# Loads of one batch reordered, and late divisions and sums moved: a fused linear-attention and feed-forward kernel

## The chip, the core and the metric

The kernel runs on one core of a Trainium2 chip. The engines are named as in the profile: PE (matmul), DVE (vector), ACT (scalar), POOL (GpSimd) and SP, which only issues DMAs here. Each engine works through its own instruction queue in order and waits on semaphores that other engines or landed DMAs raise. The metric is the device time of one execution in microseconds (us). Six runs of the kernel before gave a median of 920.74 us, from 919.83 to 923.76.

## The reference

Two stages, all in float32. The attention has no softmax: each head multiplies k and v into a 64 by 64 matrix, q is multiplied by it, and each row is divided by its root mean square. The result, seen as 4608 tokens of 512 values, goes through a two-layer network with a leaky ReLU.

```
kv  = einsum('bhsd,bhse->bhde', k, v)            # 8 batches, 8 heads, 576 rows, 64 wide
out = einsum('bhsd,bhde->bhse', q, kv)
rms = sqrt(mean(out * out, axis=-1) + 1e-6)
x   = (out / rms * g_norm) -> (4608, 512)
h   = x @ w_in                                   # 512 x 2048
out = maximum(0.01 * h, h) @ w_out               # 2048 x 512
```

## The kernel before

**Blocks.** The 4608 tokens are nine blocks of 512. While block i goes through the network, the attention of batch i+1 is done piecemeal between its matmuls. Since a batch has 576 rows, it ends in the block after the one it begins in. PE's order is written out: every matmul is pinned with `tc.keep_in_program_order`. On the other engines an instruction is pinned only where the code says so (`in_turn` pins when `steady` is set, which is from block 2 on; weight rounding, L242 to L256, is always pinned), and a scheduler puts the rest where it finds a place.

**Block 0** (`first_block`) uses plain matmuls: sixteen column groups n, each h(n) (`h_ps`, then a Prelu on ACT, line 1016) and, one step later, o(n) (`o_acc`). Between them `between(n, half)` does two things. It advances other work by one step (`steps`), and it loads and rounds weights. A weight tile comes by DMA and is rounded by two ACT instructions (L242 "add", L245 "cut") and four DVE ones (L247, L251, L253, L256). Weight tile 2n-1 serves h(n) and tile 2n+2 serves o(n). Rounding runs ahead, up to tile 31.

**Batch 1 inside block 0** is `attention(1, False)`, a generator that `steps` advances. For each half m of the heads it transposes two pairs of q (`turn`, line 426, DVE), multiplies k and v of two pairs (`attention_kv`, `kv_ps` on PE), and in half 0 it issues the loads of the third and fourth pairs (`load_pair`: k and v at line 130, q as four pieces at line 159, all on SP's queue). After half 1 come the copy of kv (line 322, DVE) and two tails. A tail is q times kv (`o_ps` on PE), squares and scaled copies on ACT (lines 350 and 356, or 395 and 400), sums of the squares on DVE (line 354 or 397), and the division. `divide` is a chain that goes to and fro: DVE transposes (line 364) and reduces (365) the sums, ACT takes the root (368), DVE the reciprocal (372), ACT spreads it (376), DVE transposes it back (382) and multiplies x (384). The division of the first tail (rows 576 to 1023, which are in block 1) falls in step n=12. The second tail's squares and sums fall in n=13, and its division is taken up in block 1 by `go(late, 1)`.

**Block 1 and later** use two levels of Strassen-like sums (seven products for eight). Their sums are made on POOL and DVE (`add`, line 598). `sides_x` makes those of x, `combine` and `sides_w1` those of the weights. From block 2 on `product_h_two` gives each of the four chunks c its h products, and the last adds of a chunk make g11, g12, g22 and g21, which ACT's Prelu (line 794) and POOL's sums (`sums_of`) take up. `product_o` does the o products of the chunk before, one step each time `go_o` is called, so that the DVE adds of both stand in one queue.

DMAs use the semaphores of eight lanes in turn, so an SP load waits until the load eight issues back has landed.

Of the kernel before, what the change touches and what calls it, by code (L numbers as in the profile page):

```python
# [23 lines left out]
def kernel(  # L24
# [46 lines left out]
    NB = B * S // NT  # L71
    N2 = NT // 2
    U = 2
    NC = DF // 2 // (U * P)
# [13 lines left out]
    ps_m = ctx.enter_context(tc.tile_pool(name="ps_m", bufs=1, space=bass.MemoryType.PSUM))  # L88

    pin = tc.keep_in_program_order  # L90
    steady = first_done = False

    def in_turn(ins):

        if steady:
            pin(ins)


# [38 lines left out]
    to_load = collections.deque()  # L137
# [281 lines left out]
    def attention(b, apart=True, fine=False):  # L419

        qT = qTs[b] = work.tile([P, NP, S], F32, tag="qT", name="qT")
        kv_ps = kv_tiles()

        def turn(p):
            q_in = q_ins.pop((b, p))
            in_turn(nc.vector.transpose(
                qT[:, p, :].rearrange("p (t s) -> p s t", s=T),
                q_in.rearrange("p (s d) -> p s d", d=D)[:, :, :32]))

        for m in range(2):  # L430
            turn(2 * m)
            yield
            turn(2 * m + 1)
            if m:
                yield
            attention_kv(b, m, kv_ps)
            pairs_next = [(b + m, p) for p in ((2, 3) if m == 0 else (0, 1)) if b + m < B]
            if apart or m == 0:
                for nxt in pairs_next[:1 if apart else 2]:
                    if apart:  # L440
                        to_load.extend((*nxt, what) for what in ("q", "kv"))
                    else:
                        load_pair(*nxt)
            yield
            if apart:
                if m:
                    copy_kv(b, kv_ps)
                for nxt in pairs_next[1:]:
                    to_load.extend((*nxt, what) for what in ("q", "kv"))
                yield  # L450
        if not apart:
            copy_kv(b, kv_ps)
            yield
        tails = [tail_of(b, max(i * NT, b * S), min((i + 1) * NT, (b + 1) * S), fine)
                 for i in (b, b + 1)]
        if not fine:
            for tail in tails:
                yield from tail
            return

        for tail in (0, 0, 0, 0, 0, 1, 0, 0, 1, 1, 1, 1, 1, 1):
            next(tails[tail])
            yield
# [133 lines left out]
    def add(eng, out_, a, b_, minus=False, pinned=False):  # L597
        ins = eng.tensor_tensor(out_, a, b_, op=ALU.subtract if minus else ALU.add)  # L598
        if pinned or steady:
            pin(ins)  # L600
# [291 lines left out]
    def product_h_two(i, c, quarters, to, second):  # L892

        n0 = 7 * ((i - 2) * NC + c)

        into = {1: (0, True), 2: (0, False), 6: (1, True), 5: (3, True), 7: (3, False),
                3: (1, False), 4: (2, True)}
        banks = {}
        for t, k in enumerate(ORDER):
            for js, tags, q in zip(GROUPS, (("ha", "hc"), ("hb", "hd")), (qa, qc)):  # L900
                tag = tags[0 if k in (1, 6, 7, 4) else 1]
                if k in FRESH:
                    banks[tag] = ps_m.tile([P, 4, P], F32, tag=tag, name=f"h_{tag}")
                for n, j in enumerate(js):
                    matmul(banks[tag][:, n, :], lhsT=w_place(n0 + t)[:, AT[j], :],
                           rhs=quarters[k][j], start=k in FRESH and n == 0, stop=True,
                           skip_group_check=True)
                if len(js) < 4 and second:
                    second.product(k, banks[tag][:, 3, :])
                at, fresh = into[k]  # L910
                bank = banks[tag][:, :len(js), :]
                if fresh:
                    nc.scalar.copy(q[:, at], bank)  # L913
                else:
                    add(nc.vector, q[:, at], bank, q[:, at])
                if len(js) < 4 and second:
                    second.done(k, banks[tag][:, 3, :])
            read(n0 + t + 1 + RING)
            yield
        g11, g21, g22, g12 = g_of(c)  # L920
        add(nc.vector, g21, qa[:, :, 0, :], qa[:, :, 1, :])
        add(nc.vector, g11, qa[:, :, 0, :], qc[:, :, 0, :])
        yield
        add(nc.vector, g22, g21, qa[:, :, 2, :])
        add(nc.vector, g12, g22, qa[:, :, 3, :])
        yield
        add(nc.vector, g22, g22, qc[:, :, 1, :])
        add(nc.vector, g21, g21, qc[:, :, 1, :])
        add(nc.vector, g21, g21, qc[:, :, 2, :])
        for t in (g11, g12, g22, g21):  # L930
            relu(t)
        sums_of(c, to)
# [47 lines left out]
    def go(steps, n=None):  # L980
        while n is None or n > 0:
            if next(steps, steps) is steps:
                return
            n = None if n is None else n - 1
# [55 lines left out]
    loaded, rounded = 7, 5  # L1040

    def between(n, half):
        nonlocal loaded, rounded
        go(steps.get(2 * n + half, iter(())), 1)

        while half and rounded < min(3 * n + 8, 2 * n + 13, len(w_jobs) - (n < 11)):
            if loaded < len(w_jobs):
                load_w(loaded)
                loaded += 1
                if loaded in (15, 19):  # L1050
                    load_pair(1, (loaded - 15) // 4)
            round_w(rounded)
            rounded += 1
        if (n, half) == (12, 0):
            for p in range(2):
                load_pair(2, p)

    first_block(between)
    first_done = True
# [35 lines left out]
    for i in range(1, NB):  # L1095
# [4 lines left out]
        for c in range(NC):  # L1100
# [3 lines left out]
            for t in range(7):  # L1104
                slot = 7 * c + t
                go(h_steps, 1)
                if not one:

                    if t == 6:
                        go(h_steps, 1)  # L1110
                    if slot in LATE_SLOTS:
                        go(late, 1)
                    for _ in range(FINE_SLOTS.get(slot, 0)):
                        go(a_steps, 1)
                    if i + 1 < NB:
                        if slot == 20:
                            x_sides, new_quarters, sums, inner = sides_x(i + 1)
                        if slot in (20, 21, 22):
                            go(sums, 2 if slot == 20 else 1)
                        if slot == 24:  # L1120
                            inner(0)
                        elif slot == 25:
                            inner(1)
                    load_some()

                now = (i - 1) * NC + c
                if now - 1 in seconds:
                    for half in range(2):
                        if t == (6 if half else 4):
                            inner_g((now - 1) % NC, half)  # L1130
                    if t == 5 and now <= 2 * NC:
                        inner_w2((now - 1) % NC)
                if slot == 4 and not one:
                    while writes:
                        pin(nc.sync.dma_start(*writes.pop()))
                if slot in HELD and i == NB - 1:
                    pass
                elif waited == LAG:
                    go_o()
                elif o_queue:  # L1140
                    waited += 1
                if one:

                    if t == 1:
                        combine(c, 2)
                    if t == 3 and c < NC - 1:
                        h_sides, more_h = sides_w1(c + 1)
                        combine(c + 1, 0)
                    if t == 5 and c < NC - 1:
                        more_h()  # L1150
                        combine(c + 1, 1)
                    if slot == 4:
                        go(late, 1)
                    if slot in A_SLOTS:
                        go(a_steps, 1)
                    load_some()
                    if slot == 24:
                        go(a_steps)
                        x_sides, new_quarters, sums, inner = sides_x(i + 1)
                        go(sums)  # L1160
                    elif slot == 25:
                        inner(0)
                    elif slot == 26:
                        inner(1)
            if i == NB - 1 and c == NC - 1:
                go(h_steps, 1)
                go_o()
            go(h_steps)
# [42 lines left out]
```

## Time and profile before

| | |
|---|---|
| median of 6 runs | 920.74 us |
| the profiled execution | 921.92 us, of which the span is 920.1 us |
| PE busy | 909.8 us (99% of the span) |
| DVE, ACT, POOL busy | 634.1, 329.3, 370.9 us |
| granted PE clock | 1.00 throughout |
| DMA | 200.06 MB, 217 GB/s over the span |

The span runs from the first to the last instruction of the program; the profiled execution's own time is 1.8 us longer. PE is the busiest engine by far, so a change is worth what it takes from, or adds to, the few places where PE stands still. Times in the views are us from the start of the span. "Idle before <-releaser" says how long the engine stood still ahead of an instruction and what ended that wait.

### The profile page before, as it was taken

To read this page: it belongs to the slowest core of one execution; us is meant where nothing else is said; L and a number is where in the kernel's file an instruction comes from. 1 tells how busy PE (TensorE), PEld (TensorE's weight loads), DVE (VectorE), ACT (ScalarE), POOL (GpSimd) and SP (SyncE) were. 2 spreads that over 40 slices of the span, in tenths; PEclk is the share of its full clock that TensorE was granted. 3 is DMA by queue.
4 is the path that set the end of the run, shared out by engine and by line. 5 is a ranking of instruction groups with operands and counts; after the bars stand their busy time and mean duration, and the time that the engine had idled before them with its cause. 6 is when DMAs were issued, how large, how long until landed. Compare 5 with 4: busy or idle time off the path is not lost.

```text
span 920.1 us, 18028 instructions
## 1 busy us (share of the span) xinstructions
PE 909.8 (99%) x6990; PEld 777.1 (84%) x6990; DVE 634.1 (69%) x1160; ACT 329.3 (36%) x649; POOL 370.9 (40%) x438
## 2 busy tenths in 40 slices
PE   8999999999999999999999999999999999999998
PEld 5444447888998999899999999999999999999997
DVE  5876995587457876687757875687569755755565
ACT  5454533242135233532343323342343333223330
POOL 2000354977633572236222632264226522642222
PEclk9999999999999999999999999999999999999999
DMA  8999936895498679856987599758765676667632
GB/s 254 235 250 224 247 106 193 267 302 166 163 343 265 185 220 294 266 178 196 295 237 230 180 285 270 227 176 251 239 182 175 189 221 199 186 186 222 199 102 92
DMA packets 90229, 200.06 MB, mean 217 GB/s; under 512 B 9888, under 2 KB 42272, under 8 KB 90144
## 3 DMA queue, kind: packets, MB, share of 16 engines
q1 hardware_dynamic: 79680, 187.04, 68.5%
q10 hardware_dynamic: 10016, 10.69, 3.3%
q8 instruction: 56, 0.92, 0.4%
q0 software_dynamic: 448, 1.18, 0.3%
q14 instruction: 29, 0.24, 0.1%
HBM read 172.39 MB, written 26.48 MB: 216 GB/s over the span
## 4 chain that ended last, share of the span: by engine, by line
PE 86%; DMA 9%; DVE 2%; POOL 1%; ACT 1%; issue 1%; SPq 0%; ACTq 0%; POOLq 0%; DVEq 0%
PE o_a L118 18%; PE o_c L118 17%; PE h_ha L118 11%; PE h_hb L118 10%; PE h_hc L118 8%; PE h_hd L118 8%; PE o_acc L118 3%; PE h_ps L118 2%; PE o_ps L118 2%; DMA stage<-in_moe_w_in_dram 2%; DMA pairs<-in_moe_w_out_dram 2%; PE kv_ps L118 2%; DMA v_in<-in_v_dram 1%; PE h_a L118 1%; DMA pairs<-in_moe_w_in_dram 1%; PE h_c L118 1%
## 5 line engine op out<-in xcount | busy, mean ns | idle before, releaser
L598 POOL TENSOR_TENSOR gs<-g 128x512 f32<-128x512 f32 x64 | 82.1, 1283 | 250.6 <-ACT g L794 248.5
L794 ACT ACTIVATE g<-g 128x512 f32<-128x512 f32 x124 | 78.4, 632 | 131.0 <-DVE g L598 131.0
L913 ACT COPY w_all<-h_ha 128x512 f32<-128x512 f32 x84 | 49.0, 583 | 171.5 <-PE h_ha L118 165.9
L118 PE MATMUL o_a<-pairs,gs 128*128 128x256 f32 x384 | 91.3, 381 | 0.0
L118 PE MATMUL o_c<-pairs,gs 128*128 128x256 f32 x376 | 89.6, 381 | 0.0
L598 DVE TENSOR_TENSOR o<-h_hb,o 128x128 f32<-128x128 f32 x104 | 29.9, 288 | 83.5 <-ACT pairs L913 83.5
L598 DVE TENSOR_TENSOR o<-o_c,o 128x512 f32<-128x512 f32 (+1 forms) x91 | 61.3, 673 | 27.6 <-PE o_c L118 27.3
L118 PEld LDWEIGHTS o_a<-pairs,gs 128*128 128x128 f32 x384 | 69.8, 190 | 10.9 <-POOL pairs L598 3.1
L118 PEld LDWEIGHTS o_c<-pairs,gs 128*128 128x128 f32 x376 | 68.3, 190 | 7.9
L598 DVE TENSOR_TENSOR o<-o_a,o 128x512 f32<-128x512 f32 x75 | 51.3, 684 | 29.1 <-PE o_a L118 28.8
L598 POOL TENSOR_TENSOR pairs<-w_all 128x512 f32<-128x512 f32 x8 | 11.1, 1382 | 121.1 <-DMA stage<-in_moe_w_in_dram 93.4
L118 PE MATMUL h_ha<-stage,w_all 128*128 128x128 f32 x448 | 59.6, 276 | 0.0
L118 PEld LDWEIGHTS h_ha<-stage,w_all 128*128 128x128 f32 x448 | 56.6, 192 | 3.0 <-issue 0.9
L118 PE MATMUL h_ps<-xT,w_all 128*128 128x512 f32 (+1 forms) x136 | 57.7, 569 | 0.7 <-DVE xT L560 0.7
L118 PE MATMUL o_acc<-w,g 128*128 128x512 f32 x128 | 57.8, 595 | 0.0
L598 POOL TENSOR_TENSOR pairs<-g 128x128 f32<-128x128 f32 x52 | 24.2, 465 | 82.0 <-PE h_hb L118 52.8
L598 DVE TENSOR_TENSOR g<-g,pairs 128x512 f32<-128x512 f32 x84 | 55.6, 689 | 1.9
L118 PEld LDWEIGHTS h_ps<-xT,w_all 128*128 128x128 f32 x136 | 25.5, 190 | 29.5 <-issue 26.3
L118 PEld LDWEIGHTS o_acc<-w,g 128*128 128x128 f32 x128 | 24.0, 190 | 29.8 <-issue 29.4
L598 DVE TENSOR_TENSOR w_all<-h_hc,w_all 128x512 f32<-128x512 f32 x56 | 38.4, 685 | 14.1 <-PE h_hc L118 13.8
L598 DVE TENSOR_TENSOR o<-h_hd,o 128x128 f32<-128x128 f32 x78 | 22.2, 284 | 36.7 <-ACT pairs L913 36.2
L118 PE MATMUL h_hb<-stage,w_all 128*128 128x128 f32 x336 | 46.7, 275 | 0.0
(225 smaller groups left out, 2267.7 us busy)
## 6 DMA issues: line engine op xcount, KB each, us to landing
w_all<-w SPq DMA_DIRECT2D x196, 448.0 KB, 4.3
pairs<-w SPq DMA_DIRECT2D x56, 512.0 KB, 4.3
out_dram<-o ACTq DMA_DIRECT2D x35, 256.0 KB, 5.4
v_in<-in_v_dram SPq DMA_DIRECT2D x29, 288.0 KB, 5.1
k_in<-in_k_dram SPq DMA_DIRECT2D x28, 288.0 KB, 5.2
q_in<-in_q_dram SPq DMA_DIRECT2D x56, 144.0 KB, 6.1
q_in<-in_q_dram SPq DMA_DIRECT2D x56, 140.0 KB, 6.1
w<-stage SPq DMA_DIRECT2D x12, 512.0 KB, 4.4
```

The lines of the kernel that those rows point to most:

```text
L118: pin(nc.tensor.matmul(*args, **kw))
L598: ins = eng.tensor_tensor(out_, a, b_, op=ALU.subtract if minus else ALU.add)
L794: nc.scalar.activation(t, t if src is None else src, func=AF.Prelu, alpha=SLOPE)
L913: nc.scalar.copy(q[:, at], bank)
```

## The change

Five edits:

- In half 0 of `attention(1, False)` k and v of the third and of the fourth pair are issued first, and then q of both. Before, it was k, v, q of the third and then k, v, q of the fourth.
- `in_turn` also pins when a new flag `in_line` is set. `between` sets it while it advances `steps` for n of 12 and more: the first tail's division and the second tail's sums then stay in program order among the pinned DVE instructions, behind the rounding of all weight tiles.
- The second tail's division is taken up at slot 5 of block 1, not at slot 4, and is pinned too.
- `product_h_two` yields once more, ahead of the last two adds of g21.
- At the very last chunk `go(h_steps, 1)` and `go_o()` are called twice and not once, so that an o add comes between the last adds.

```
-    steady = first_done = False
+    steady = first_done = in_line = False
     def in_turn(ins):
-        if steady:
+        if steady or in_line:
             pin(ins)
...
             if apart or m == 0:
-                for nxt in pairs_next[:1 if apart else 2]:
-                    if apart:
-                        to_load.extend((*nxt, what) for what in ("q", "kv"))
-                    else:
-                        load_pair(*nxt)
+                for nxt in pairs_next[:1] if apart else ():
+                    to_load.extend((*nxt, what) for what in ("q", "kv"))
+                if not apart:
+                    for what in ("kv", "q"):
+                        for nxt in pairs_next:
+                            load_pair(*nxt, what)
...
         add(nc.vector, g22, g22, qc[:, :, 1, :])
+        yield
         add(nc.vector, g21, g21, qc[:, :, 1, :])
         add(nc.vector, g21, g21, qc[:, :, 2, :])
...
     def between(n, half):
-        nonlocal loaded, rounded
+        nonlocal loaded, rounded, in_line
+        in_line = n >= 12
         go(steps.get(2 * n + half, iter(())), 1)
+        in_line = False
...
-                    if slot == 4:
+                    if slot == 5:
+                        in_line = True
                         go(late, 1)
+                        in_line = False
...
-            if i == NB - 1 and c == NC - 1:
+
+            for _ in range(2 if i == NB - 1 and c == NC - 1 else 0):
                 go(h_steps, 1)
                 go_o()
             go(h_steps)
```

## The prediction

> **What bounds the kernel now.** I read the PE waits first, because PE is 99% busy. PE stands still for few causes; the three that the edits touch are these (total us, times, longest).
>
> ```profile
> PE kv_ps L118 <- DMA v_in<-in_v_dram: 1.9, 1, 1.9
> ...
> PE h_b L118 <- ACT g L819: 0.4, 1, 0.4
> ...
> PE o_c L118 <- DVE o L598: 0.4, 1, 0.4
> ```
>
> Next the chain that ended last (start, us, what), to see which waits set the end. v of batch 1's fourth pair is on it at 81.42. So is v of batch 2's fourth pair at 164.83. The h_b wait at 159.56 is not: there the chain runs through POOL's sums and SP.
>
> ```profile
> 81.42 8.08 DMA v_in<-in_v_dram
> 89.50 0.14 issue
> 89.63 1.27 PE kv_ps L118 x70
> ...
> 164.83 5.65 DMA v_in<-in_v_dram
> 170.48 0.04 issue
> 170.53 1.27 PE kv_ps L118 x70
> ```
>
> SP's timeline shows the loads that move: four pieces of q of the third pair stand ahead of k and v of the fourth.
>
> ```profile
> 77.08 2.23 SPq L159 DMA_DIRECT2D q_in<-in_q_dram  x4
> 79.63 0.35 SPq L130 DMA_DIRECT2D k_in<-in_k_dram  x1
> 81.42 0.35 SPq L130 DMA_DIRECT2D v_in<-in_v_dram  x1
> 82.94 3.02 SPq L159 DMA_DIRECT2D q_in<-in_q_dram  x4
> ```
>
> DVE's timeline decides the case. From 100.80 to 140 DVE is idle for one wait of 1.58 us only. Its operations are stretched where POOL adds run: L253 takes 1.76 here and 0.69 elsewhere, while the transposes (L382) keep their 0.63.
>
> ```profile
> 100.80 0.60 DVE L247 TENSOR_SCALAR cut<-cut 128x512 f32<-128x512 f32 x1
> ...
> 123.04 1.76 DVE L253 SCALAR_TENSOR_TENSOR w<-cut,w 128x512 uint32<-128x512 uint32 x1
> ...
> 128.67 0.63 DVE L382 STREAM_TRANSPOSE inv<-spread 128x448 f32<-128x448 f32 x1
> ...
> 131.34 1.21 DVE L256 CUSTOM_DVE_ANT_0 w<-w,add 128x1024 uint16<-128x1024 uint16 x1
> ```
>
> ACT's timeline: the second tail's square waits for that transpose. The Prelus of h(14) at 130.18 and h(15) at 135.35 stand behind it, and both are early or on time.
>
> ```profile
> 129.39 0.39 ACT L395 ACTIVATE sq<-o_ps 128x256 f32<-128x256 f32 x1 [5.27 <-DVE inv L382]
> 129.67 0.62 ACT L400 ACTIVATE xT<-o_ps,g_sb 128x128 f32<-128x128 f32 x2
> 130.18 0.61 ACT L1016 ACTIVATE g<-h_ps 128x512 f32<-128x512 f32 x1
> 135.35 0.60 ACT L1016 ACTIVATE g<-h_ps 128x512 f32<-128x512 f32 x1 [4.57 <-PE h_ps L118]
> ```
>
> **What the Trainium skill says.** "SBUF — State Buffer", section "Who interferes with whom": DVE and POOL share a pair of ports under an exclusive lock; a DVE operation with two SBUF inputs or in a two-port mode, and a POOL one that reads SBUF, block each other for a whole instruction. The trace agrees: L253's 1.76 is the end of a POOL add (124.25) plus 0.55. "PSUM — Partial Sum Buffer", section "Engine vs sequencer instructions": the queues of ACT, DVE and POOL are strict FIFO, and matmuls start in program order. So a Prelu behind a waiting square is late, however ready; the trace shows it at 130.18. "DMA: Bandwidth & Descriptors", section "Queues, rings and completion order": descriptors are consumed in ring order, but completion is not promised in order. Here k, v and q take about the same 6 to 8 us from issue to landing, so I take landings in issue order.
>
> **Edit 1, the loads.** k or v is 288 KB, a pair's q 568 KB (twice 144 + 140). The windows give 254 and 210 GB/s around 80, so 230 in the mean: q takes 2.5 us. Moved ahead of one q, v lands at 89.50 - 2.5 = 87.0. PE comes to these matmuls at 87.41 and stood until 89.63, so 2.2 us of PE go (the waits view books 1.9, the modelled end of two matmuls being later). The k and v buffers were released by matmuls at 70.1, so SP can issue at 77.08, where q stood. q of the third pair lands 2.6 us later, still with that of the fourth; both are first read at 98.24, seven or so us after landing. The bytes in total are the same, so the weights behind them move little. If the landing is not in order, the gain is anything down to 0.
>
> **Edit 2, what the scheduler made of it.** PE's order is the same in both kernels. On ACT the Prelus of h(10) and h(11) and the four `o_ps` instructions of the first tail now come ahead of the rounding of tile 25; before, tiles 25 and 26 were rounded at 98.50 between the two Prelus. All DVE rounding now precedes the division. I follow the chain.
>
> - PE's first-tail products move from 104.77 to 102.57. ACT took from 105.86 to 107.77 for their squares and copies; now 103.66 to 105.57. The two ACT roundings (107.77 to 109.00 before, for tile 27) then end at 106.80, and DVE starts tile 25 at 106.84, not 100.80. DVE's transposes end at 100.95 in both, so nearly 6 us of a full DVE are lost.
> - DVE's work up to the second inverse transpose: 100.80 to 132.55 is 31.75, less the 1.58 wait, less the second multiply (1.61, which now comes after): 28.56. This gives 135.4.
> - Nothing covers the trips to ACT any more: root 0.32 and one spread 0.56 with some 0.2 of semaphores: 1.1. This gives 136.5.
> - The lock: 16 POOL adds (5 from 99.83, 11 from 122.15) fall in the stretch in both kernels. Before, some met transposes or the wait and cost nothing. Alone, the 28.56 would be about 21.5 (seven tiles at 2.25, the rest 5.8), so the lock cost 7. If every add cost its full price (8 large ones at 1.0, 8 small at 0.5) it would be 12. So the extra is 0 to 5, and below 0 by some 2 if adds fall on DVE's waits. With rounding in one piece, I take 1.2: the second inverse transpose ends at 137.7.
> - ACT then: squares and copies of the second tail, 0.9 for each half (129.39 to 130.30), the first half from 0.55 before that transpose's end; then the Prelu of h(15), 0.6, now behind them. It ends 1.8 after the transpose, at 139.5.
> - o(15) starts on PE at 139.55. Before: 135.32 + 3.43 = 138.75. PE itself would have been there at 136.55. So PE stands 3.0, and block 1 begins 0.8 later than before: edit 1's gain is spent.
>
> x is needed by block 1's first matmuls 3.4 us after that; the second multiply and the sums of x (some 2.5 us) fit.
>
> **Edit 3, slot 5.** DVE's h_c add comes ahead of the small division, so ACT's copy at 158.85 is not held up and the 0.43 wait goes. It pays nothing: PE only arrives earlier at the kv matmuls, whose v is set by POOL's sums that start when h_c ends (149.1), SP's queue and the landing at 170.48. h_d's add, now behind the division, has until 163.09.
>
> **Edits 4 and 5, the end.** Now DVE does three g adds (898.38 to 900.39) and then the o_c add (900.31 to 900.99); PE's next o_c matmuls wait for it from 900.69 to 901.14. With one g add ahead the o_c add ends at 899.7, and the 0.45 goes. The last g add ends 0.6 later, POOL's four sums likewise (second one at 904.4), but PE needs that one at 907.7. After that PE runs to the end: -0.45 is in full. Its cover gone, the same wait would stand elsewhere, down to 0.
>
> **Sum.** +0.8 + 0 - 0.45 = +0.35. The profiled execution's own 921.92 would be 922.3. It lies 1.2 above the median of the runs shown and within their spread, so I put the same +0.35 on the median: 921.1.
>
> **The rivals.** (a) Faster: the division is in time. It needs the inverse transpose by 134.75, so the lock must cost 1.75 less than before, not 1.2 more. Then -2.2 - 0.45 gives 918.1. For it: PE is otherwise full, and POOL's adds may fall on DVE's waits; against it: 6 us less of DVE. (b) Slower: POOL's adds meet rounding one for one. From an inverse transpose at 139.2 on (an extra of 2.7) the kernel is more than 0.2% slower; at an extra of 3.4 o(15) starts at 141.75, +3.0 - 0.45, 923.3. For it: eleven POOL adds follow each other from 122.15, right where rounding now stands undivided. (c) The loads don't do what they say: v lands as late as before, PE keeps its wait, and the lost DVE time comes on top, all 2.2 later: 923.3. Against it: q's pieces land within 7 us of their issue.
>
> **How the numbers follow.** About 0.2% (1.8 us) is what a measurement can tell from no change. Forecast 0.57 (its own range 919.3 to 922.5), (a) 0.14, (b) 0.23, (c) 0.06. So faster 0.14, same 0.57, slower 0.29. The range takes in most of (a) and all of (b) and (c): 918.6 to 923.8.
>
> **What would show it.** Right: no PE wait on `v_in` near 87; DVE idle for 5 to 6 us from 101; a new PE wait ahead of `o_acc` near 137 of about 3 us, ended by ACT's Prelu, with squares (L395) and DVE's L382 before it; the h_b wait gone but kv_ps still held by v near 171; no o_c wait near 900. Wrong: no wait ahead of the last `o_acc` (then a), one of over 5 us (then b), or a wait that I don't see in block 1's first sums.

## The result and the profile after

The changed kernel takes 927.11 us in the median of 16 runs (925.77 to 928.9), the kernel before 920.93 of 35 on the same chips. The ratio is 1.0064, 95% interval 1.0054 to 1.0075: slower by 5.0 to 6.9 us. The prediction, 921.1 with a range of 918.6 to 923.8, was wrong. The profiled execution of the changed kernel took 926.33 us, with a span of 924.6, 4.5 above the span before.

PE's waits in the changed kernel (total us, times, longest). Those for `v_in`, h_b and o_c, shown of before, are gone. In their place stands one.

```profile
PE o_acc L118 <- ACT g L1018: 5.3, 1, 5.3
```

The chain of waits shown of before went through v's landing twice. After, it goes through neither: from 107.26 on it runs along DVE's rounding and the division to ACT's squares, copies and Prelu, and from there to o(15).

```profile
142.25 5.89 PE o_acc L118 x8
```

SP's timeline: k and v of the fourth pair are issued ahead of q (the window ends ahead of the eighth piece of q).

```profile
75.57 0.33 SPq L130 DMA_DIRECT2D k_in<-in_k_dram  x1
76.12 0.33 SPq L130 DMA_DIRECT2D v_in<-in_v_dram  x1
76.68 6.36 SPq L159 DMA_DIRECT2D q_in<-in_q_dram  x7
```

PE's timeline shows their products, 72 instructions in one piece where before two stood apart from 70, and then o(14), o(15) and the first h_a of block 1. First the o products and that h_a of before, then the changed kernel:

```profile
135.16 7.03 PE L118 MATMUL o_acc<-w,g 128*128 128x512 f32 x16
142.02 1.89 PE L118 MATMUL h_a<-xT,w_all 128*128 128x256 f32 x8
```

```profile
87.84 1.28 PE L118 MATMUL kv_ps<-v_in,k_in 64*64 64x64 f32 x72
...
133.37 3.60 PE L118 MATMUL o_acc<-w,g 128*128 128x512 f32 x8
142.25 5.89 PE L118 MATMUL o_acc<-w,g 128*128 128x512 f32 x8 [5.29 <-ACT g L1018]
147.98 1.89 PE L118 MATMUL h_a<-xT,w_all 128*128 128x256 f32 x8
```

The line of 142.25 and the one after it hold the loss. A group of eight such matmuls takes 3.43 us from its start to the next start (before, sixteen took 6.86). So PE is ready for o(15) at 136.80, the start of o(14) plus 3.43, and starts at 142.25. Then the eight matmuls take 5.73 us, start to start.

DVE's timeline: it is idle from 101.45 and takes up tile 25 at 107.26. Its operations are stretched while POOL adds run (L253 takes 1.64 against 0.69 elsewhere, and ends 0.55 after the POOL add that started at 108.78), and the second inverse transpose ends at 140.55.

```profile
107.26 0.43 DVE L247 TENSOR_SCALAR cut<-cut 128x512 f32<-128x512 f32 x1 [5.81 <-ACT cut L245]
...
109.14 1.64 DVE L253 SCALAR_TENSOR_TENSOR w_all<-cut,w_all 128x512 uint32<-128x512 uint32 x1
...
138.22 0.65 DVE L382 STREAM_TRANSPOSE inv<-spread 128x448 f32<-128x448 f32 x1 [0.63 <-ACT spread L376]
...
139.91 0.64 DVE L382 STREAM_TRANSPOSE inv<-spread 128x448 f32<-128x448 f32 x1
```

```profile
108.78 1.45 POOL L599 TENSOR_TENSOR pairs<-w 128x512 f32<-128x512 f32 x1
110.31 1.59 POOL L599 TENSOR_TENSOR pairs<-w,pairs 128x512 f32<-128x512 f32 x1
```

ACT's timeline: the rounding (L242) stands behind the squares of the first tail (L350), and the Prelu of h(15) at 141.57 behind the squares and copies of the second, which wait for DVE.

```profile
104.08 0.98 ACT L350 ACTIVATE sum<-o_ps 128x448 f32<-128x448 f32 x2 [0.39 <-PE o_ps L118]
...
105.98 0.69 ACT L242 ACTIVATE add<-pairs 128x512 uint32<-128x512 uint32 x1
...
140.02 0.39 ACT L395 ACTIVATE sq<-o_ps 128x256 f32<-128x256 f32 x1 [1.37 <-DVE xT L384]
...
141.57 0.63 ACT L1018 ACTIVATE g<-h_ps 128x512 f32<-128x512 f32 x1
```

To see where time goes in all kernels alike, I cut PE's timeline at four starts that each kernel has: the kv matmuls of batch 1's third and fourth pair, the o matmul behind them, block 1's first h_a, and the h_d behind the second kv matmuls of block 1. In us; the four columns after the first run from one of these starts to the next, the last of them to the end of the span:

| | kv starts | kv takes | to block 1 | to h_d | to the end | span |
|---|---|---|---|---|---|---|
| before | 87.41 | 3.43 | 51.18 | 29.71 | 748.37 | 920.1 |
| after | 87.84 | 1.21 | 58.93 | 28.87 | 747.75 | 924.6 |
| difference | +0.43 | -2.22 | +7.75 | -0.84 | -0.62 | +4.5 |

The 0.43 lies ahead of all edits; over the executions profiled here the kv matmuls start anywhere from 87.36 to 88.78. The 7.75 are the 5.45 that PE stands ahead of o(15) and the 2.30 that o(15) is slow.

### The profile page after: what moved, and what is told of

Same layout as the page of the kernel before. It is cut to its first block, busy times and chain, and to the rows that moved or that the text cites. A ratio compares the mean times of both kernels' runs of the same rounds, so it can differ in the third digit from the quotient of the medians.

```text
span 924.6 us, 18027 instructions
## 1 busy us (share of the span) xinstructions
PE 911.7 (99%) x6990; PEld 778.0 (84%) x6990; DVE 634.9 (69%) x1160; ACT 329.7 (36%) x649; POOL 370.3 (40%) x438
## 4 chain that ended last, share of the span: by engine, by line
PE 84%; DMA 7%; DVE 6%; ACT 1%; issue 1%; SPq 0%; POOL 0%; DVEq 0%; ACTq 0%; POOLq 0%
PE o_a L118 19%; PE o_c L118 18%; PE h_ha L118 11%; PE h_hb L118 10%; PE h_hc L118 8%; PE h_hd L118 8%; PE o_ps L118 2%; PE kv_ps L118 2%; PE h_a L118 2%; PE h_b L118 1%; DMA q_in<-in_q_dram 1%; PE h_c L118 1%; PE h_d L118 1%; DMA pairs<-in_moe_w_in_dram 1%; DMA pairs<-in_v_dram 1%; DMA k_in<-in_k_dram 1%
## 5 line engine op out<-in xcount | busy, mean ns | idle before, releaser
L118 PE MATMUL o_acc<-w,g 128*128 128x512 f32 x128 | 60.3, 615 | 5.3 <-ACT g L1018 5.3
```

The costliest lines, as they stand in the source:

```text
L118: pin(nc.tensor.matmul(*args, **kw))
```

## The experiments

**One edit at a time.** My prediction put the reordering on ACT under edit 2, the pins. Four kernels take edits 1 and 2 apart. Edit 1 alone:

```
-                for nxt in pairs_next[:1 if apart else 2]:
...
+                    for what in ("kv", "q"):
+                        for nxt in pairs_next:
+                            load_pair(*nxt, what)
```

> The kernel before with edit 1 alone. Theory A (edit 1 itself makes the scheduler put ACT's rounding of tiles 25 and 26 behind the first tail's squares, and the pins only move the division): the PE wait for v near 87 goes (-2.2 us), DVE stands still some 6 us from 101, and with the division in the midst of the rounding tile 29 is ready near 135.4 instead of 129.7, so PE stands 5 to 6 us ahead of h(15) and a little more ahead of o(14): 924 to 928 us. Theory B (my prediction: the pins of edit 2 move ACT's rounding): DVE keeps working from 101, and only the 2.2 us go: 918.7.

Edit 2 alone:

```
-        if steady:
+        if steady or in_line:
...
+        in_line = n >= 12
         go(steps.get(2 * n + half, iter(())), 1)
+        in_line = False
```

> The kernel before with edit 2 alone. Theory A: ACT rounds tiles 25 and 26 at 98.5 as before and DVE has no idle time from 101. The division comes after all rounding, the second inverse transpose ends near 134.5 and the last Prelu of block 0 near 136.3, ahead of the 138.75 at which PE comes to o(15): 920.9, within 0.6 of the kernel before. Theory B (the pins cause the 6 us of idle DVE): the Prelu ends near 142.2 as in the changed kernel, PE stands 3.4 us, plus 2.3 of slower matmuls: near 926.5.

The changed kernel without edit 2 in block 0:

```
-        in_line = n >= 12
+        in_line = False
```

> The changed kernel without edit 2 in block 0 (the flag is not set in between; slot 5 keeps its pin). Theory A: as edit 1 alone, with the gains of slot 5 (0.4 to 0.8) and of the end (0.45): 923 to 927, PE standing ahead of h(15) and not ahead of o(15). Theory B: 917.5, no wait of PE near 137.

The changed kernel without edit 1:

```
-                    for what in ("kv", "q"):
-                        for nxt in pairs_next:
-                            load_pair(*nxt, what)
...
+                for nxt in pairs_next[:1 if apart else 2]:
...
+                        load_pair(*nxt)
```

> The changed kernel without edit 1 (the loads in their old order; edits 2 to 5 stay). Theory A, as the run of edit 1 alone and that of edit 2 alone have left it (edit 1 reorders ACT, the pins alone cost less than 1 us): ACT rounds tiles 25 and 26 near 98.5, DVE has no idle time of 5.8 us from 101, PE stands less than 1 us ahead of o(15) and the clock stays at 1.00: 920 to 922, and the wait for v near 87 is back. Rival (each edit is enough with the others): PE stands over 3 us ahead of o(15), over 925.

| | ratio to before (95%) | kv takes | to block 1 | to h_d | to the end |
|---|---|---|---|---|---|
| edit 1 alone | 1.0075 (1.0058 to 1.0092) | 1.21 | 60.88 | 30.03 | 748.34 |
| edit 2 alone | 1.0003 (0.9987 to 1.0019) | 2.23 | 52.25 | 29.30 | 748.44 |
| all but edit 2 | 1.0079 (1.0060 to 1.0099) | 1.21 | 58.31 | 29.41 | 747.73 |
| all but edit 1 | 1.0010 (0.9991 to 1.0029) | 2.71 | 52.27 | 29.58 | 747.70 |

DVE's timeline of edit 1 alone, tile 25, and then of edit 2 alone, tile 25 and the one wait after it:

```profile
107.55 0.43 DVE L247 TENSOR_SCALAR cut<-cut 128x512 f32<-128x512 f32 x1 [5.81 <-ACT cut L245]
```

```profile
102.21 0.59 DVE L247 TENSOR_SCALAR cut<-cut 128x512 f32<-128x512 f32 x1
...
109.21 0.43 DVE L247 TENSOR_SCALAR cut<-cut 128x512 f32<-128x512 f32 x1 [1.30 <-ACT cut L245]
```

Theory A holds in its cause, and with it falls my assignment. The reordered loads themselves made the scheduler put ACT's rounding of tiles 25 and 26 behind the first tail: DVE's 5.81 us of idle time are there without a pin, and not there with pins alone. Why the scheduler does so, no run shows. Edit 1 alone, and the changed kernel with or without edit 2, are slower by amounts that their runs can't tell apart (1.0064 to 1.0079), and without edit 1 the runs show no loss. Edit 2 only decides who is late: without it the rounding itself, as PE's waits in edit 1 alone show.

```profile
PE o_acc L118 <- DVE w L256: 4.3, 1, 4.3
PE h_ps L118 <- DVE w_all L256: 2.3, 1, 2.3
```

The places I had partly wrong: 5 to 6 us ahead of h(15) and a little ahead of o(14) were expected, and it is 2.3 and 4.3. The medians of edit 1 alone and of all but edit 2, both 928.6, lie up to 1.6 us above the ranges given; the kernel before took 921.97 beside them.

By itself edit 2 costs 1.07 us of PE ahead of block 1 in the trace (the Prelu of h(14) then stands behind the second tail's copies), too little for its runs to tell from none.

**Edit 3 alone, and edits 4 and 5 alone.**

```
-                    if slot == 4:
+                    if slot == 5:
                         go(late, 1)
```

> The kernel before with edit 3 alone (slot 5, without a pin). My prediction's step: the h_b wait of 0.43 us goes and PE stands as much longer at the kv matmuls near 170: 920.9. Theory A (as the changed kernel shows, 0.84 us less from the first h_a of block 1 to the end of those matmuls): the kv wait goes too: 920.1 to 920.5.

```
         add(nc.vector, g22, g22, qc[:, :, 1, :])
+        yield
...
-            if i == NB - 1 and c == NC - 1:
+            for _ in range(2 if i == NB - 1 and c == NC - 1 else 0):
```

> The kernel before with edits 4 and 5 alone. My prediction's step: the o_c wait of 0.45 us near 900 goes, nothing else moves: 920.5, 0.45 below the kernel before. Rival: the wait stands elsewhere in the last chunk: 920.9.

Neither differs from before in its runs: the ratios are 1.0006 (0.9988 to 1.0023) and 0.9997 (0.9977 to 1.0017). The trace is finer. With edit 3 alone the h_b wait is gone, PE waits 1.21 at the kv matmuls near 170, and the stretch to h_d is 30.14, not below the 29.71 of before: my step was right, and the 0.84 that the changed kernel gains there is not edit 3's own. There v is issued 22.42 after block 1's first product, against 22.81 before, and PE, which comes to these matmuls 27.40 after that product, is not seen to wait for it. That block 1 begins late does not explain it: in edit 1 alone it begins at 150.23, later still, and PE waits 0.43 for v. Why v's way is shorter by some tenths no run shows. With edits 4 and 5 the last stretch is 747.67 to 747.75 in every kernel that has them, and 748.34 to 748.44 in the four that don't: 0.6 to 0.8 us.

**The slow o(15).** PE's windows of the changed kernel (us, busy, granted clock, DMA share, GB/s): the clock is halved from just before 140, while PE still stands, for two times 3.4 us.

```profile
139.00:139.90 0.90, 0.00 (x0) 0.98 0.00 0
140.00:143.40 3.40, 1.15 (x2) 0.50 0.00 0
143.40:146.80 3.40, 3.40 (x6) 0.51 0.14 52
146.90:150.00 3.10, 3.10 (x13) 1.00 0.77 268
```

The Trainium skill says, in "TensorE: Matmul & The Clock Gate", section "Part 1: The HAM clock gate", that PE's clock is halved after an idle window of about 3.4 us and given back after a busy one, and that these windows run freely. The lengths agree: the clock is low for two stretches of 3.4 us, and full again after one, 143.40 to 146.80, in which PE was busy throughout. The fall came sooner than a whole window without work: near 139.9 PE had stood for 2.9 us. To show that standing still is the cause, matmuls that nothing reads fill the wait:

```
             between(n, 0)
+            if n == 2 * NC * U:
+                idle = ps_m.tile([P, NT], F32, tag="ha", name="idle_ps")
+                for _ in range(11):
+                    matmul(idle, lhsT=ident, rhs=x[:, 0, :], start=True, stop=True)
```

> The changed kernel with eleven more matmuls of 512 columns into an idle PSUM bank, just ahead of o(15): work that nothing reads, put where PE stands still for 5.3 us. Theory A (PE's granted clock falls because PE stood still, and the eight o(15) matmuls take 5.7 instead of 3.4 us for that): the wait is filled, o(15) starts within 0.5 us of where it did and takes 3.4 to 3.6 us, 924.8. Rival (the eight matmuls are slow for another reason, such as what DVE and POOL do then): o(15) takes 5.7 us still, 927 to 927.5.

Eleven were too many: in the trace one is two instructions and takes 0.86 us, so they filled 9.44 us, o(15) came 3.5 us later than in the changed kernel and the ratio was 1.0074 (1.0054 to 1.0093). Its o(15) took 3.43 and the clock stayed at 1.00. With `range(6)`:

> The changed kernel with six matmuls into an idle bank ahead of o(15) instead of eleven: one takes 0.87 us in the run with eleven, which filled 9.5 us where only 5.3 were free. Theory A (standing still lowers PE's clock): the six fill 5.2 us, PE starts o(15) as soon as the Prelu has ended, within 0.3 of the changed kernel, the eight matmuls take 3.4 to 3.6 us and not 5.7, and block 1 begins 2.3 us earlier: 924.8. Rival: the eight take 5.7 us still: 927.

PE's timeline with six:

```profile
136.56 5.31 PE L118 MATMUL idle_ps<-xT,ident 128*128 128x512 f32 x12
142.00 3.70 PE L118 MATMUL o_acc<-w,g 128*128 128x512 f32 x8
145.53 1.89 PE L118 MATMUL h_a<-xT,w_all 128*128 128x256 f32 x8
```

From o(15) to block 1 it is 3.53 us and not 5.73; the stretch to block 1 falls from 58.93 to 56.72, by 2.21. The ratio is 1.0041 (1.0025 to 1.0056), 2.1 us below the 1.0064. So the clock is shown: 2.2 to 2.3 us of the loss up to block 1, on top of the wait. Not all of it is kept: in this trace the stretch to h_d is 30.57 and not 28.87, with waits of 0.73 ahead of block 1's third product and of 0.67 for v.

**POOL's adds.** In `add`, for block 0's sums on POOL (the sums are left out):

```
+        if lean and eng is nc.gpsimd:
+            eng.memset(out_, 0.02)
+            return
```

> The changed kernel with POOL's sixteen sums of block 0 (of weights, for block 1) replaced by fills of the same tiles with a constant, so that POOL writes as much but reads nothing; the sums are left out. Theory A (DVE's operations are stretched by POOL's adds, in all by some 10 us between tile 25 and the second inverse transpose): that stretch falls from 33.3 to 22 to 24 us, the last Prelu of block 0 is in time, PE does not stand ahead of o(15): 918 to 919.5. Rival (the stretching has another cause): the stretch stays at 32 or more and the time at 927.

The ratio is 0.9974 (0.9960 to 0.9989), the span 917.5, with 51.18 to block 1: PE waits nowhere in that stretch. DVE's timeline:

```profile
107.30 1.30 DVE L247 TENSOR_SCALAR cut<-cut 128x512 f32<-128x512 f32 x1 [5.80 <-ACT cut L245]
...
120.84 0.61 DVE L247 TENSOR_SCALAR cut<-cut 128x512 f32<-128x512 f32 x1 [1.58 <-ACT cut L245]
...
133.58 0.64 DVE L382 STREAM_TRANSPOSE inv<-spread 128x448 f32<-128x448 f32 x1
```

DVE starts as late as in the changed kernel, but the stretch to the second inverse transpose is 26.92 instead of 33.29, and 1.58 of the 26.92 are a wait for ACT. So POOL's adds cost DVE 8.0 us more than the fills do; I expected a stretch of 22 to 24 and had counted neither this wait nor that fills stretch DVE too (1.30 for 0.43). Fills are also shorter than adds (for 128 by 512 values some 0.5 to 0.7 us against 1.3 to 1.7), so the run tells what the adds cost, not whether it is their reads or their length.

**Where DVE's lateness goes.** First, the Prelu's place on ACT: the second tail later.

```
-                 for i in (12, 13, 15, 16, 18, 20, 22, 23, 24, 26, 28))
+                 for i in (12, 13, 15, 16, 18, 20, 22, 23, 24, 30, 31))
```

> The changed kernel with the second tail taken up two steps of n later (keys 30 and 31 instead of 26 and 28). DVE's order stays the same; on ACT the Prelu of h(15) now stands ahead of the second tail's squares and copies, behind the two spreads. Theory A (the Prelu is late because it stands behind squares that wait for DVE's inverse transposes): the Prelu ends near 138.8, PE stands 1.5 to 2 us ahead of o(15) and up to 1 us more ahead of the first sums of block 1, and the matmuls keep their speed: 921 to 923. Rival (what counts is that DVE is late with x, and the Prelu's place only decides where PE stands): PE stands 5 us ahead of block 1 instead: 926 to 927.

PE stands 2.21 ahead of o(15), and 2.76 more ahead of block 1's third product, whose first matmuls run at half clock. The ratio is 1.0044 (1.0022 to 1.0066), near what the rival expected: the Prelu's place decides mainly where PE stands. Next, the first tail later, so that DVE starts earlier (`24, 25, 26, 27, 28` for `22, 23, 24, 26, 28`):

> The changed kernel with the first tail of batch 1 taken up two steps later (keys 24, 25, 26 instead of 22, 23, 24) and the second's at 27. The scheduler then puts ACT's rounding of tiles 25 and 26 ahead of the first tail's squares, but still behind the Prelu of h(11), and the Prelu of h(15) ahead of the second tail's squares. Theory A (DVE's late start is what costs): DVE starts tile 25 near 104.8 instead of 107.3, the second inverse transpose ends near 138.1, PE stands less than 1 us near 137 and up to 1 us ahead of block 1's first sums, and the gains of edit 1 and slot 5 show: 917.5 to 920. Rival (POOL's adds then stretch DVE as much more as it starts earlier): the transpose ends at 140 or later, 923 to 926.

DVE starts tile 25 at 105.33, but the transpose ends at 141.27, as the rival had it: the first tail's sums now come behind all rounding, stretched too, and ACT lets DVE wait 1.84 once more. PE stands 2.1 ahead of o(15) and 1.0 ahead of block 1's third product, the clock stays at 1.00 in the profiled execution, and the ratio is 1.0017 (0.9999 to 1.0036). It is the best of the kernels that keep edit 1 and leave nothing out. DVE's end is no earlier for it. What it gains on the changed kernel lies in PE's waits: the Prelu of h(15) now stands ahead of the second tail's squares, and neither wait was followed by half clock. It does not beat the kernel before.

Then POOL's sums were moved, not left out:

```
-        if pinned or steady:
+        if pinned or steady or behind and eng is nc.gpsimd:
             pin(ins)
...
+    x_row = block(1)[:, 0, S - NT:S - NT + 8]
...
+    behind = True
+    gate = work.tile([P, 8], F32, name="gate", tag="gate")
+    add(nc.gpsimd, gate, x_row, x_row)
     for part in range(2):
         sides_w2(0)[1](part)
     for part in range(2):
         combine(0, part)
+    behind = False
```

> The changed kernel with twelve of POOL's sixteen sums of block 0 (four of w_out, eight of w_in for block 2) moved behind a small POOL add that reads x of the first tail's first rows after its multiply, into the stretch from 135.7 to 155.1 in which POOL has nothing to do. Nothing is left out, and the order on DVE, ACT, PE and SP stays the same. Theory A (DVE is late by its late start and by the adds that meet its rounding): between tile 25 and the second inverse transpose DVE loses 5 to 7 us of stretching and gets a wait for ACT of up to 1.6, so that the transpose ends near 135 instead of 140.6; the last Prelu is in time, PE stands less than 1 us ahead of o(15), the clock stays at 1.00, and edit 1's 2.2 us show: 918 to 920, below the kernel before. Rival (the sums are late for block 1, or stretch DVE's sums of x as much): PE stands ahead of block 1's products that read them, 922 to 926.

The ratio is 1.0055 (1.0030 to 1.0080): a miss. DVE did nearly as expected (the second transpose ends at 136.54, not near 135), and PE stood 1.16 ahead of o(15), but then 4.9 us in block 1, with half clock from within this wait until after it. PE's waits put this down to POOL's sums:

```profile
PE h_a L118 <- POOL stage L599: 4.9, 1, 4.9
```

The last of POOL's sums ended at 149.51, 0.8 ahead of PE's start at 150.31. ACT's copy of the same bank, at 149.62, ended at 150.21, 0.1 ahead of it. It stood behind ACT's copies of o, and these behind DVE's copies of o, behind operations of DVE that POOL stretched (the second tail's sums, L397, 2.62 for 0.48). The next run gates POOL behind the third sum of x (`x_sides[7]` in place of `x_row`), 4 us later:

> As the run that moved twelve POOL sums, but behind the third sum of x for block 1 instead of the first tail's multiply, so that they start near 139.8 and not at 136.2 and meet none of DVE's multiplies and sums of x. Theory A (the 4.9 us ahead of block 1's third h_a product in that run was ACT's copy of the bank at 149.62, late because DVE's copies of o stood behind operations that POOL stretched): the copies of o are in time, that wait is under 0.5 us, PE stands about 1.2 us ahead of o(15), the clock stays at 1.00, block 1 begins 0.8 below the kernel before: 918.5 to 920.5. Rival (PE waits for POOL's sums themselves, as the view of waits names it): POOL ends 3 us later, and so does the wait: over 930.

This wait is gone, although POOL's sums end 2.7 us later: PE waited for ACT's copy, not for POOL's sums. But PE's waits have another:

```profile
PE h_a L118 <- DVE g L599: 1.9, 1, 1.9
```

DVE stood 3.69 us at 153.16 for the DMA that empties a place of `stage`, which POOL had filled late, and its g sums came late; PE's clock is halved again after this wait. And PE waits 1.65 for v of batch 2, which SP issues 27.0 us after block 1's first product and not 22.4, behind the DMAs of POOL's late sums. The ratio is 1.0034 (1.0018 to 1.0049). The same with the second tail at keys 30 and 31:

> As the run with POOL's twelve sums behind the third sum of x, and the second tail taken up at keys 30 and 31, so that the Prelu of h(15) stands ahead of its squares on ACT. Theory A: the Prelu ends near 135.5, PE stands nowhere between 90 and 140, and edit 1's 2.2 us are left in full: 917 to 919, below both kernels. Rival: the squares and copies, now behind the Prelu, make x late for block 1 and PE stands there: 919.5 or more.

The stretch to block 1 is 51.18: the 2.2 us of edit 1 are there in full at block 1's start. More than that is given back after it (waits of 1.09 and 1.97, and of 2.67 for v), and the ratio is 1.0034 (1.0021 to 1.0046). No kernel here that computes all of it beats the one before.

## Why the prediction was wrong

- **Edit 1's own gain: right.** v was taken to land at 87.0 and the 2.2 us to go. It lands near 84.1 (issued at 76.12, 8.0 on its way), with 3.7 to spare: SP came to k and v at 75.57 and 76.12, not at 77.08. The kv matmuls take 1.20 or 1.21 in every kernel with edit 1, and 2.23 to 4.91 without it (4.91 with a halved clock).
- **Edit 2, "what the scheduler made of it": wrongly assigned, though rightly foreseen for both together.** DVE was to start at 106.84; it starts at 107.26, later by the 0.43 that lie ahead of the edits. But edit 1 does this, not the pins. The total didn't suffer from that; a reader who drops the pins to get rid of the loss would keep it.
- **"The lock ... I take 1.2": the term that failed.** 107.26 to 140.55 is 33.29; less the trips to ACT (1.02, predicted 1.1) and my 28.56, it leaves 3.7 and not 1.2. In edit 2 alone, where DVE starts at 102.21 (kv 1.4 later than before), it is 32.28 - 1.30 of waiting - 1.01 - 28.56 = 1.4. So 1.2 was about the price with an early start. The traces show where the rest arises, in POOL's first five adds: by an estimate from DVE's durations beside them and elsewhere, they stretch DVE by 5.0 us in the changed kernel, where all five meet rounding and sums, and by 3.0 in edit 2 alone, where the first two fall mostly on transposes and a copy; the other eleven stretch it by 5.7 and 5.3. A part of the error is in the reading of before: the 16 adds do not all fall in the stretch from 100.80 to 132.55, as the prediction has it. One starts ahead of it, three behind it; in the changed kernel all 16 fall inside. My bound of 5 held, my choice inside it did not. Less the 0.43, the transpose came 2.4 later than predicted; PE stood 5.45 and not 3.0. That the late start is what raises the price is read from these traces; the run with the first tail later, in which DVE starts 1.9 earlier, did not lower it.
- **Not in the sum at all: the clock.** The sum has no term for what follows a stand-still. It cost 2.30 more in o(15), of which the run with six idle matmuls gets back 2.2 there.
- **A slip without consequence.** The 138.75 for o(15) of before comes from a start in the chain's view, 135.32; the timeline has 135.16, and so 138.59.
- **Edit 3: right alone**, as shown; in the changed kernel this stretch was 0.84 shorter, and v did not hold the kv matmuls near 171 as predicted. The cause stays open.
- **Edits 4 and 5: right in kind, 0.65 and not 0.45.** The view books 0.45, from a modelled end of matmuls; start to start the wait was 901.14 - 898.80 - 1.73 = 0.61.
- **The sum**: -2.22 + 5.45 + 2.30 - 0.84 - 0.62 = +4.07, and 0.43 ahead of the edits: +4.5, the difference of the spans. The medians differ by 6.2, as the profiled execution of before was 1.0 over its median and that of after 0.8 under its own.
- **Rival (b)** had mechanism, place and size of the wait: an extra of 3.4 with o(15) at 141.75 (142.25 less 0.43 is 141.82). It had a chance of 0.23; its 923.3 lacked the clock, and it looked for the cost in the eleven late adds rather than in the first five. Rivals (a) and (c) are excluded by the wait at o(15) and by the kv matmuls.

## What to carry to other kernels

A transfer moved in the program is also new input to the scheduler: compare the order on every engine for each edit by itself before assigning an effect to one. When an engine is full, price a late start at what it then overlaps, add by add, not at the mean of the old place. A stand-still of the bound engine is to be priced with the slow clock behind it, and a wait that is removed from a chain this tight shows up at the next link unless that link has slack too, as it did in the runs that moved POOL's sums.

## What the runs showed of the hardware

The halved clock also follows waits of PE that are shorter than the idle window of about 3.4 us that the Trainium skill gives in "TensorE: Matmul & The Clock Gate", section "Part 1: The HAM clock gate", and not each of them; here the measurement decides. After 2.51 us of waiting for v in the run of edits 4 and 5, PE ran at half clock, as this window shows.

```profile
91.50:94.80 3.30, 3.30 (x72) 0.50 0.95 251
```

Likewise it did after 2.29 ahead of h(15) in the run without pins, after 1.94 in the run that gates POOL behind the third sum of x, and around the end of 2.76 in the first run with the second tail at keys 30 and 31. After 1.90 in the kernel before, 2.27 in edit 1 alone, 2.63 in the run without pins and 2.67 in the last run above it did not. So between 1.9 and 2.8 us the length of the wait does not decide. In three of the four halved cases the clock fell 0.1 to 0.6 us after PE had started again, in the fourth 0.2 ahead. Each halving lasted about 3.4 us, or twice that after the waits of 4.3 to 5.3.

This also bears on how the kernel before scatters. Of its 184 runs beside the experiments, 123 have a mean granted clock of at least 0.999, with a median of 921.3 us; 33 have 0.998, which is what one halving of 3.4 us makes of the mean, with 924.7; and 28 have less, with 927.2. All five kernels with the old order of loads have runs below 0.999 (besides these 61 of 184: 4 of 22, 4 of 14, 10 of 22 and 10 of 22). Of the three with edit 1 in which PE stands no longer than 1.5 us (both with idle matmuls, and the one with fills) none of the 33 runs is below 0.999. So the wait for v near 87 probably costs the kernel before a halving in about a third of its executions, which edit 1 takes away; it is seen as it happens only in the one trace of edits 4 and 5.
